# Two spectral-mixing and MLP layers: stores of made weight parts on ScalarE's DMA queue, issued two product steps after the part is complete, with the raw loads behind them

## The chip, the cores and the metric

One core of a Trainium2 chip runs the whole program. The metric is device time in microseconds of one execution; the kernel before was run three times. TensorE is called PE, VectorE DVE, ScalarE ACT, GpSimd POOL and SyncE SP in the profile. SP does no arithmetic here: it only issues DMAs.

## The reference, cut to what matters

```python
# x [2048, 576]; w1 [576, 4608]; w2 [4608, 576]; everything f32
def A(y):                                  # spectral mixing
    a, b = y @ dft_hid_re.T, y @ dft_hid_im.T
    return dft_seq_re @ a - dft_seq_im @ b
def B(y):                                  # MLP, gelu in its tanh form
    return gelu(y @ w1 + b1) @ w2 + b2
x = x + A(layernorm(x))
x = x + B(layernorm(x))
x = x + A(layernorm(x))
x = x + B(layernorm(x))
```

The two layers use the same w1, w2 and DFT matrices.

## The kernel before

**Products.** Each large matrix product is cut in 2 x 2 blocks and computed by a scheme of seven block products in place of eight (numbered 1 to 7; `ORDER` is the order in which a group of seven runs). For this, sums and differences of blocks are formed on both sides ("parts"). Each operand of TensorE is then split in two fp32r numbers, a high part (a copy by ScalarE) and a low part (the operand less the high part, a subtraction by VectorE), and a product is three passes of matmuls: high x high, high x low, low x high. A *part* of a weight is therefore a tile in `R` that holds high and low, and it has to be made once: raw blocks are loaded, POOL forms the sum or difference, ScalarE writes the high part, VectorE the low part. The finished parts of w1 and w2 are stored to DRAM scratch (`w1s`, `w2s`, both called `w_parts` in the profile, w1_parts and w2_parts in the lists of instructions) and loaded again by the later halves, so that the making is paid for once, in the first layer. `R` is the store of fp32r tiles and `A` that of f32 tiles, `bank` is PSUM.

**Stages.** Each layer has a *sequence stage* (class `Sequence`; the DFT along 2048 rows: 14 tiles after two opening ones, seven products each, of 24 matmuls 128x288; method `run`, from L663), then, for each of two halves of the rows, `hidden` (the DFT along 576 columns, the residual, the layer norm, transposes by TensorE) and `mlp` (L1015). The halves are interleaved: the last transposes of `hidden` (generator `turn_y`, taken step by step from L998 to L1003) stand among the first products of `mlp`.

**The MLP.** w1 is worked in 18 steps q, w2 in 9 groups g. `inner(q)` runs seven products of seven matmuls 128x512, adds up their banks (VectorE, `add`, L193), and makes GELU (ScalarE) and the parts of its result. `outer(g, i)` runs product i of the second matrix, in two half products of 12 matmuls 128x288 (one for each result tile of 128x576). Iteration g of the loop does: first inner (q = 2g), first outer (products 1, 6, 5, 3 of group g-1), second inner (q = 2g+1), second outer (products 7, 4, 2 of group g-1). A counter `at` numbers the places of an iteration: 0 to 6 the products of the first inner, 7 to 14 the half products of the first outer, 15 to 21 the second inner, 22 to 27 the second outer. PE runs the matmuls in this order of the code; a half product's result is taken out of its bank by VectorE's L193 add.

**What is made in the background.** Two makers run beside this work, and both put instructions into the same ScalarE, VectorE and SP queues.

- `weights()` (L249 on) makes the 126 parts of w1, 7 for each of 18 q. It is a generator; a step n writes the low of part n-1 (`low`, one VectorE subtraction L196, and at once the store of 128x640 and, in four of seven steps, the load of a raw block for q+1, 128x384) and the high of part n (`high`, L269 and L270 on ScalarE). Its parts lie in a ring `stage` of three slots, `n % 3`. `pump()` takes one step. `tick(3)` after each product of the first sequence stage (L694) pumps after three products of four; `tick(2)` in `inner` (L1161) after every second product; and `load_w` (L1030), which loads a w1 part for the MLP, pumps until that q's parts are made.
- `make(g)` (L1055), used only in the first half of the first layer (`first`), makes the seven w2 parts of group g: `hi` on ScalarE (L1061), `lo` on VectorE (L196, 128x576) with its store of 128x1152 behind it, then POOL's next difference and, in four of seven, the raw load for the next group (`load_raw`, L1051). A table of places says when: parts 1, 5, 6 at 0 to 5 (the first inner), 3 at 9 and 10, and 7, 4, 2 at 15 to 20 (the second inner). `advance()` (L1083) runs what is due at a place.

```python
        def low(n):
            ...
            sub(nc.vector, t[:, 0:5:2], cut(src), t[:, 1:4].bitcast(F32))
            dma(w1s[q, i - 1], at(n).bitcast(F32))
...
            return list(zip((0, 1, 2, 3, 4, 5, 9, 10, 15, 16, 17, 18, 19, 20),
                            one + five + six + three + seven + four + two))
```

**The DMA queue.** `dma` (L189, L190) is `nc.sync.dma_start`: all loads and stores of the kernel, 1347 of them, are issued by SP, in the order of the code. An issue waits in SP for whatever its tile or its data need, and all later issues wait behind it. Eight semaphores (DMAHW0 to DMAHW7 in the lists) are taken in turn, and an issue also waits for the earlier one that has its semaphore.

**The second layer's sequence stage** is prepared in pieces while the first layer's last MLP half still runs: `prepare` and `fill` (generators; L327 to L462) are moved on by `next(before)` in the last six inners (L1163). A piece loads, normalizes, or writes highs (ScalarE, L499 to L511) or lows (VectorE).

## Time and profile before

| what | value |
| --- | --- |
| median of three runs | 2736.05 us (2735.36 to 2740.49) |
| the profiled execution's own time | 2739.99 us |
| its span, first to last instruction | 2737.9 us |
| granted clock of TensorE, mean | 0.996 |
| PE busy (matmul) | 2669.0 us, 97% |
| PEld busy (weight load, beside PE) | 2500.1 us, 91% |
| DVE busy | 1772.6 us, 65% |
| ACT busy | 1101.3 us, 40% |
| POOL busy | 790.6 us, 29% |
| DMA | 544.91 MB, mean 199 GB/s |
| the first layer's sequence stage, about | 60 to 390 us |
| its first MLP half (w2 is made), about | 455 to 910 us |
| the second layer's sequence stage begins at about | 1350 us |

How to read it: a line of the groups has the code line, engine, operation, written tile <- read tiles, shape and count, then the busy time and the mean of one in ns, then the idle time of that engine just before these instructions with what ended most of it. TensorE's waits are listed as "who waits <- what released it: total us, count, longest". Rows of the chain of waits start with a time and a duration; SPq is SP's DMA issuing. Rows of the timeline read: start, duration, engine, line, instruction; a count x stands for that many instructions put together, and a bracket holds the wait ahead of it. In the stretches each engine has busy time and count, in the order PE, PEld, DVE, ACT, POOL, and then the granted clock, the share of the DMA engines' time and GB/s. DMA rows end with the median us from issue to landing.

### The profile page before, as it was taken

How to read it: one execution, taken by the hardware profiler on the slowest of the kernel's cores; microseconds unless marked ns; L12 is line 12 of the kernel's file. 1: busy time of each engine (PE TensorE's matmuls, PEld its weight loads, DVE VectorE, ACT ScalarE, POOL GpSimd, SP SyncE). 2: the span in 40 equal slices, each digit the busy share in tenths (PEclk: the TensorE clock that was granted, in tenths of full speed). 3: DMA queues.
4: the chain of work that ended last, by engine and by line, in shares of the span. 5: the costliest groups of instructions: out<-in, count | busy, mean ns of one | idle time of the engine just before them, and what ended most of it. 6: DMA issues, size and time to landing. Idle time of an engine off the chain costs nothing.

```text
span 2737.9 us, 45326 instructions
## 1 busy us (share of the span) xinstructions
PE 2669.0 (97%) x17488; PEld 2500.1 (91%) x17488; DVE 1772.6 (65%) x2582; ACT 1101.3 (40%) x1838; POOL 790.6 (29%) x746
## 2 busy tenths in 40 slices
PE   7999999999999999999999999999999999999999
PEld 7999998788888988988899999998989899898988
DVE  8788866777776575556566666565555556655555
ACT  6555545544443243333344333344333324433331
POOL 5222224543534432213241000042222224222222
PEclk9999999999999999999999999999999999999999
DMA  5666675777777546667463333536666673666664
GB/s 201 233 224 223 227 259 189 268 263 269 270 259 254 201 153 193 191 197 222 156 220 120 122 124 122 201 104 209 193 194 193 195 256 129 200 193 195 192 194 153
DMA packets 209286, 544.91 MB, mean 199 GB/s; under 512 B 22048, under 2 KB 56864, under 8 KB 208928
## 3 DMA queue, kind: packets, MB, share of 16 engines
q1 hardware_dynamic: 209072, 542.02, 60.2%
q8 instruction: 138, 2.26, 0.3%
q14 instruction: 76, 0.62, 0.1%
HBM read 429.87 MB, written 114.72 MB: 199 GB/s over the span
## 4 chain that ended last, share of the span: by engine, by line
PE 68%; DVE 5%; issue 3%; DMA 3%; POOL 2%; ACT 1%; SPq 0%; POOLq 0%; DVEq 0%; ACTq 0%
PE bank L203 67%; DVE R L196 2%; DMA R<-w_parts 2%; DVE A L193 1%; PE bank L818 1%; POOL A L196 1%; DVE A L196 1%; DVE bank L193 1%; POOL R L196 0%; DMA A<-in_c 0%; DMA w_parts<-R 0%; SPq L190 0%; ACT R L1179 0%; DVE moments L233 0%; ACT A L243 0%
## 5 line engine op out<-in xcount | busy, mean ns | idle before, releaser
L203 PE MATMUL bank<-R 128*128 128x288 f32 (+2 forms) x16972 | 2621.7, 316 | 56.1 <-DVE A L193 14.4
L203 PEld LDWEIGHTS bank<-R 128*128 128x128 f32 x16972 | 2445.8, 189 | 222.2 <-DVE A L193 24.2
L193 DVE TENSOR_TENSOR A<-bank,A 128x576 f32<-128x576 f32 (+3 forms) x808 | 566.7, 709 | 555.3 <-PE bank L203 473.0
L196 POOL TENSOR_TENSOR R<-A,R 128x512 fp32r<-128x512 f32 x288 | 374.5, 1311 | 951.8 <-ACT R L1179 912.2
L196 DVE TENSOR_TENSOR R<-A,R 128x1024 fp32r<-128x1024 f32 (+10 forms) x521 | 495.5, 975 | 61.0 <-ACT R L615 25.5
L193 POOL TENSOR_TENSOR A<-A 128x576 f32<-128x576 f32 (+2 forms) x102 | 135.9, 1334 | 633.0 <-ACT A L653 350.2
L1117 ACT ACTIVATE bank<-bank,b1t 128x512 f32<-128x512 f32 (+1 forms) x224 | 144.7, 646 | 372.0 <-DVE bank L193 256.5
L1179 ACT ACTIVATE R<-A 128x512 fp32r<-128x512 f32 x288 | 176.1, 629 | 279.0 <-DVE A L196 118.1
L615 ACT ACTIVATE R<-A 128x1024 fp32r<-128x1024 f32 x196 | 204.0, 1054 | 135.3 <-DVE A L196 105.9
L193 DVE TENSOR_TENSOR bank<-bank,A 128x512 f32<-128x512 f32 (+1 forms) x228 | 152.0, 669 | 151.1 <-PE bank L203 150.8
L196 DVE TENSOR_TENSOR R<-bank,R 128x512 fp32r<-128x512 f32 x336 | 210.1, 639 | 56.9 <-ACT R L199 48.0
L196 POOL TENSOR_TENSOR A<-A 128x384 f32<-128x384 f32 (+2 forms) x154 | 194.4, 1270 | 180.4 <-DVE R L196 90.9
L196 DVE TENSOR_TENSOR A<-A 128x1024 f32<-128x1024 f32 (+3 forms) x132 | 136.6, 1040 | 6.1 <-ACT A L243 2.1
L1144 ACT ACTIVATE A<-bank 128x512 f32<-128x512 f32 (+1 forms) x76 | 43.7, 575 | 233.2 <-PE bank L203 230.5
L1179 ACT ACTIVATE R<-bank 128x512 fp32r<-128x512 f32 x216 | 120.6, 596 | 32.9 <-PE bank L203 32.9
L196 DVE TENSOR_TENSOR A<-bank,A 128x512 f32<-128x512 f32 x144 | 97.9, 680 | 0.0
L199 ACT ACTIVATE R<-bank 128x512 fp32r<-128x512 f32 (+1 forms) x112 | 50.4, 492 | 92.6 <-PE bank L818 85.1
L243 ACT ACTIVATE A<-A,moments 128x576 f32<-128x576 f32 x64 | 53.7, 863 | 57.4 <-POOL moments L226 28.4
L655 DVE SCALAR_TENSOR_TENSOR A<-A 128x288 f32<-128x288 f32 x28 | 18.4, 657 | 88.8 <-POOL A L193 88.8
L1117 ACT ACTIVATE A<-bank,b1t 128x512 f32<-128x512 f32 (+1 forms) x76 | 50.5, 664 | 52.9 <-DVE bank L193 52.8
L270 ACT ACTIVATE R<-A,power,middle 128x128 fp32r<-128x128 f32 x126 | 60.8, 483 | 0.0
L269 ACT ACTIVATE R<-A 128x256 fp32r<-128x256 f32 x126 | 51.3, 407 | 14.0 <-DMA A<-in_w 10.8
(58 smaller groups left out, 613.6 us busy)
## 6 DMA issues: line engine op xcount, KB each, us to landing
R<-w_parts SPq DMA_DIRECT2D x504, 320.0 KB, 3.4
R<-w_parts SPq DMA_DIRECT2D x189, 576.0 KB, 3.7
A<-in_cs SPq DMA_DIRECT2D x112, 512.0 KB, 4.3
w_parts<-R SPq DMA_DIRECT2D x126, 320.0 KB, 4.0
w_parts<-R SPq DMA_DIRECT2D x63, 576.0 KB, 3.9
uv_mid<-A SPq DMA_DIRECT2D x32, 576.0 KB, 2.8
A<-in_w SPq DMA_DIRECT2D x72, 192.0 KB, 3.9
R<-dh_parts SPq DMA_DIRECT2D x23, 576.0 KB, 8.2
```

Source lines behind the costliest of these rows:

```text
L193: engine.tensor_tensor(dst, a, b, op=op)
L196: engine.tensor_tensor(dst, a, b, op=OP.subtract)
L199: nc.scalar.activation(hi, src, AF.Copy)
L203: nc.tensor.matmul(o, a, b, start=start, stop=stop, skip_group_check=True)
L243: nc.scalar.activation(dst, src, AF.Identity, bias=mv[:, 4:5], scale=mv[:, 3:4])
L269: nc.scalar.activation(t[:, 1:4:2], src[:, 0:3:2], AF.Copy)
L270: nc.scalar.activation(t[:, 2], src[:, 1], AF.Identity, bias=power[:, 2:3], scale=middle)
L615: nc.scalar.activation(self.cells[t, i](2, NP, P)[:, 0], self.source(t, i), AF.Copy)
L818: nc.tensor.transpose(at, v[:, k], ident)
L1117: nc.scalar.activation(dst, src, AF.Gelu_apprx_tanh, bias=bias(f))
L1144: nc.scalar.activation(up, o, AF.Copy)
L1179: nc.scalar.activation(H[q, k](2, TC)[:, 0], src, AF.Copy)
```

## The change

It has five parts.

1. **w1 stores.** A new helper `put` issues a DMA from ScalarE's queue. In `weights()` the store, the raw load (still SP) and the note that a q is made move out of `low(n)` into `keep(n)`, which runs two steps later: step n now runs `keep(n-2)`, `low(n-1)`, `high(n)`. The ring still has three slots.
2. **w1 steps in the sequence stage.** `tick(3)` becomes `pump()` after every product but product 2: six steps for seven products, 84 of the 126 in the stage where there were 73 or 74.
3. **w2 parts.** In `make` stores and raw loads go through `soon`: into a list `kept`, issued by `advance` two places later, stores through `put`. Parts 1 and 5 of the next group are made at places 24 to 27 of the iteration before (in the second outer), 6 at 0 and 1, 3 at 9 and 10, and 7, 4, 2 at 15 to 20 as before. For the first group 1, 5 and 6 stay together (0 to 5); the last group's 6, 3, 7, 4, 2 stand at 5 to 14.
4. **Pieces of the second sequence stage.** `high_parts` is cut in `high_left` and `high_z`, `low_parts(1)` in `low_z` and `right_sums`, with yields between; `lv` becomes a list of blocks, and the load of the second pair's left block leaves earlier.
5. **Last transposes.** The steps of `turn_y(3)` taken between the first MLP products are 0, 3, 3 where they were 1, 2, 3.

```diff
@@ -189,6 +189,9 @@
+    def put(dst, src):
+        nc.scalar.dma_start(dst, src)
+
     def add(engine, dst, a, b, op=OP.add):
@@ -275,9 +278,13 @@
             sub(nc.vector, t[:, 0:5:2], cut(src), t[:, 1:4].bitcast(F32))
-            dma(w1s[q, i - 1], at(n).bitcast(F32))
             if then:
                 then()
+
+        def keep(n):
+
+            q, k = divmod(n, 7)
+            put(w1s[q, steps[k][0] - 1], at(n).bitcast(F32))
             if k in (2, 4, 5, 6):
@@ -286,8 +293,10 @@
         yield
-        for n in range(7 * NQ + 1):
-            if n:
+        for n in range(7 * NQ + 2):
+            if n > 1:
+                keep(n - 2)
+            if 0 < n <= 7 * NQ:
                 low(n - 1)
@@ -351,7 +360,7 @@
                     yield
-            self.lv = Block(A, EARLY_X[2], 8 * P)(1, 8, P)
+            self.lv = [Block(A, EARLY_X[2], 8 * P)(8, P)]
             self.load_left(0)
@@ -370,23 +379,25 @@
                     yield
-                self.high_parts(0)
+                self.high_left(0)
+                yield
+                self.high_z(0)
                 yield
                 self.low_left(0)
+                self.lv = self.left_blocks()
+                self.load_left(1)
                 yield
...
                 yield
-            self.lv = Block(A, L_AT, NP * 8 * P)(NP, 8, P)
             if self.early:
                 self.t = Block(A, EARLY_T, 2 * D)
-                self.load_left(1)
-                yield
                 self.right_sums(0)
...
             else:
+                self.lv = self.left_blocks()
                 self.has_left(1)
@@ -418,9 +429,12 @@
                     self.low_left(1)
+                    yield
                     self.low_sums(0)
                     yield
-                    self.low_parts(1)
+                    self.low_z(1)
+                    yield
+                    self.right_sums(1)
                     yield
@@ -433,7 +447,11 @@
                         self.load_left(k)
-                if p + 1 < NP:
+                if p == 0 and self.early:
+                    self.high_left(1)
+                    yield
+                    self.high_z(1)
+                elif p + 1 < NP:
                     self.high_parts(p + 1)
@@ -460,6 +478,11 @@
+        def left_blocks(self):
+
+            v = Block(A, L_AT, NP * 8 * P)(NP, 8, P)
+            return [v[:, p] for p in ((0, 2, 1, *range(3, NP)) if self.early else range(NP))]
+
         def has_left(self, k):
@@ -484,7 +507,7 @@
             for t in range(PLAIN):
-                dma(self.lv[:, p, 4 * t:4 * t + 4], c0[p][:, t])
+                dma(self.lv[p][:, 4 * t:4 * t + 4], c0[p][:, t])
@@ -496,14 +519,17 @@
         def high_left(self, p):
-            nc.scalar.activation(self.left(p)[:, 0], self.lv[:, p], AF.Copy)
+            self.parts[p] = self.own.take()
+            nc.scalar.activation(self.left(p)[:, 0], self.lv[p], AF.Copy)
...
+            self.high_left(p)
+            self.high_z(p)
+
+        def high_z(self, p):
+
             v, z = self.x[p], self.Z[p](7, 2, DH)
-            if p not in self.parts:
-                self.parts[p] = self.own.take()
-                self.high_left(p)
             if p not in self.normal:
@@ -525,7 +551,7 @@
             c = self.left(p)
-            sub(nc.vector, c[:, 1], self.lv[:, p], c[:, 0].bitcast(F32))
+            sub(nc.vector, c[:, 1], self.lv[p], c[:, 0].bitcast(F32))
@@ -691,7 +717,8 @@
                     hidden.begin(self, ORDER.index(i))
-                tick(3)
+                if i != 2:
+                    pump()
             for k in range(2):
@@ -996,7 +1023,7 @@
         y_steps = turn_y(3)
-        for n in (1, 2, 3):
+        for n in (0, 3, 3):
             next(mlp)
@@ -1043,7 +1070,7 @@
-        due = []
+        due, kept = [], []
         if first:
@@ -1063,24 +1090,28 @@
                 sub(nc.vector, t[:, :, 1], src, t[:, :, 0].bitcast(F32))
-                dma(w2s[g, i - 1], got2[g, i](2, 2 * DH).bitcast(F32))
+                b = got2[g, i]
+                soon(lambda: put(w2s[g, i - 1], b(2, 2 * DH).bitcast(F32)))
+
+            def soon(step):
+                kept.append((at[1] + 2, step))
...
             six = [lambda: hi(6, x), lambda: (lo(6, x), sub(pool, x, b21, x))]
-            five = [lambda: hi(5, b11), lambda: (lo(5, b11), load_raw(g + 1, 0))]
-            three = [lambda: hi(3, b22), lambda: (lo(3, b22), sub(pool, b12, b22, b12), load_raw(g + 1, 2))]
-            seven = [lambda: hi(7, b12), lambda: (lo(7, b12), load_raw(g + 1, 1))]
+            five = [lambda: hi(5, b11), lambda: (lo(5, b11), soon(lambda: load_raw(g + 1, 0)))]
+            three = [lambda: hi(3, b22), lambda: (lo(3, b22), sub(pool, b12, b22, b12), soon(lambda: load_raw(g + 1, 2)))]
+            seven = [lambda: hi(7, b12), lambda: (lo(7, b12), soon(lambda: load_raw(g + 1, 1)))]
             four = [lambda: hi(4, x), lambda: lo(4, x)]
-            two = [lambda: hi(2, b21), lambda: (lo(2, b21), load_raw(g + 1, 3))]
-            if g == NG - 1:
-                return list(zip((1, 2, 5, 6, 7, 8, 9, 10, 12, 13, 14, 15, 16, 17),
-                                one + six + five + three + seven + four + two))
-            return list(zip((0, 1, 2, 3, 4, 5, 9, 10, 15, 16, 17, 18, 19, 20),
-                            one + five + six + three + seven + four + two))
-
-        at = [0]
+            two = [lambda: hi(2, b21), lambda: (lo(2, b21), soon(lambda: load_raw(g + 1, 3)))]
+            late = (5, 6, 7, 8, 9, 10, 11, 12, 13, 14) if g == NG - 1 else (0, 1, 9, 10, 15, 16, 17, 18, 19, 20)
+            return list(zip((24, 25, 26, 27), one + five)), list(zip(late, six + three + seven + four + two))
+
+        at = [0, 0]
         def advance(to=None):
+            at[1] += to is None
+            while kept and kept[0][0] <= at[1]:
+                kept.pop(0)[1]()
             while due and due[0][0] <= (at[0] if to is None else to):
@@ -1251,7 +1282,14 @@
             if first and g:
-                due.extend(make(g - 1))
+                if g == 1:
+                    soon, late = make(0)
+                    due.extend((n, step) for n, (_, step) in enumerate(soon))
+                    late[:2] = [(n + 4, step) for n, step in late[:2]]
+                due.extend(late)
+                if g < NG:
+                    soon, late = make(g)
+                    due.extend(soon)
             if g == NG:
@@ -1274,6 +1312,8 @@
                         outer(g - 1, i, 1 - f)
+        for _, step in kept:
+            step()
         for s in (c2, tmps):
```

In the MLP's group 4, second inner, SP's rows read before (lines L190 are the helper `dma`; the last row is the load of the w1 part for the inner's seventh product):

```order
L190 DMA w1_parts<-R_66 128x640 [waits DMAHW0_49,DVE_49]
L190 DMA A_67<-in_w1 128x384 [waits DMAHW1_49]
L190 DMA R_66<-w1_parts 128x640 [waits DMAHW2_49,PE_49]
L190 DMA w2_parts<-R_66 128x1152 [waits DMAHW3_49,DVE_49]
L190 DMA A_67<-in_w2 128x2x288 [waits DMAHW4_49]
L190 DMA R_66<-w1_parts 128x640 [waits DMAHW5_49,PE_49]
```

After the change the same place of SP's queue, with the same load as the last row:

```order
L190 DMA A_67<-in_w1 128x384 [waits DMAHW2_49,DVE_49]
L190 DMA R_66<-w1_parts 128x640 [waits DMAHW3_49,PE_49]
L190 DMA R_66<-w1_parts 128x640 [waits DMAHW5_49,PE_49]
L190 DMA A_67<-in_w2 128x2x288 [waits DMAHW0_49,DMAHW4_49,DVE_49,Pool_49]
L190 DMA R_66<-w1_parts 128x640 [waits DMAHW1_49,PE_49]
L190 DMA R_66<-w1_parts 128x640 [waits DMAHW7_49,DMAHW3_49,PE_49]
```

Both stores have left SP's queue, and the raw load of w2 (in_w2) no longer stands directly ahead of the load; another w1 load stands between.

On ScalarE, in the first sequence stage, one product's rows before (L269 and L270 are `high`, L615 and L645 the stage's own work):

```order
L645 ACTIVATE A_67<-bank_68 128x288 [waits DVE_49,PE_49]
L269 ACTIVATE R_66<-A_67 128x2x128 [waits DMAHW4_49,Pool_49]
L270 ACTIVATE R_66<-A_67,power_70,middle_72 128x128 [waits Activation_49]
L615 ACTIVATE R_66<-A_67 128x1024 [waits Activation_49]
L269 ACTIVATE R_66<-A_67 128x2x128 [waits DMAHW5_49,DMAHW7_49,DVE_49,Activation_49]
```

and after (L193 is now `put`; `high` is L272 and L273):

```order
L193 DMA w1_parts<-R_66 128x640 [waits DVE_49,Activation_49]
L272 ACTIVATE R_66<-A_67 128x2x128 [waits DMAHW6_49,Pool_49]
L273 ACTIVATE R_66<-A_67,power_70,middle_72 128x128
L641 ACTIVATE R_66<-A_67 128x1024 [waits DVE_49]
L193 DMA w1_parts<-R_66 128x640 [waits Activation_49]
L272 ACTIVATE R_66<-A_67 128x2x128 [waits DMAHW1_49,Pool_49]
```

The store of a part stands in ScalarE's own queue now, ahead of the next high, and that high waits for a DMA semaphore.

On VectorE, at the end of an iteration (second outer) and the start of the next one's first inner, before (L193 the adds out of the banks, L196 subtractions):

```order
L196 TENSOR_TENSOR R_66<-bank_68,R_66 128x512
L196 TENSOR_TENSOR A_67<-bank_68,A_67 128x512 [waits DVE_49]
L193 TENSOR_TENSOR A_67<-bank_68,A_67 128x576 [waits PE_49]
L196 TENSOR_TENSOR R_66<-bank_68,R_66 128x512 [waits Activation_49]
L196 TENSOR_TENSOR A_67<-A_67,bank_68 128x512
L193 TENSOR_TENSOR A_67<-bank_68,A_67 128x576 [waits PE_49] x2
```

and after (the same helpers are L196 and L199):

```order
L199 TENSOR_TENSOR R_66<-bank_68,R_66 128x512
L199 TENSOR_TENSOR A_67<-bank_68,A_67 128x512 [waits DVE_49]
L199 TENSOR_TENSOR R_66<-A_67,R_66 128x2x288 [waits DMAHW0_49,Activation_49]
L196 TENSOR_TENSOR A_67<-bank_68,A_67 128x576 [waits PE_49]
L199 TENSOR_TENSOR R_66<-bank_68,R_66 128x512 [waits Activation_49]
L199 TENSOR_TENSOR A_67<-A_67,bank_68 128x512
L196 TENSOR_TENSOR A_67<-bank_68,A_67 128x576 [waits PE_49]
L199 TENSOR_TENSOR R_66<-A_67,R_66 128x2x288 [waits DMAHW7_49,Activation_49]
L196 TENSOR_TENSOR A_67<-bank_68,A_67 128x576 [waits PE_49]
```

The two rows of 128x2x288 are the lows of w2 parts 1 and 5 of the next group; they stood in the next iteration's first inner.

## The prediction

> **What bounds the kernel now.** I read the page first, then TensorE's waits, the chain of waits, busy time by stretch, and last the timeline at the places where TensorE stood.
>
> ```profile
> span 2737.9 us, 45326 instructions
> L203 PE MATMUL bank<-R 128*128 128x288 f32 (+2 forms) x16972 | 2621.7, 316 | 56.1 <-DVE A L193 14.4
> L615 ACT ACTIVATE R<-A 128x1024 fp32r<-128x1024 f32 x196 | 204.0, 1054 | 135.3 <-DVE A L196 105.9
> L270 ACT ACTIVATE R<-A,power,middle 128x128 fp32r<-128x128 f32 x126 | 60.8, 483 | 0.0
> L269 ACT ACTIVATE R<-A 128x256 fp32r<-128x256 f32 x126 | 51.3, 407 | 14.0 <-DMA A<-in_w 10.8
> ```
>
> The matmul line stands idle for 56.1 us of 2737.9, so TensorE is the bound and no change of waits can win more than some 2%. Where those waits lie:
>
> ```profile
> PE bank L203 <- DMA R<-w_parts: 8.6, 9, 2.4
> PE bank L203 <- DVE A L193: 8.1, 13, 1.1
> PE bank L203 <- DVE bank L193: 7.1, 7, 2.2
> ...
> 653.26 9.01 PE bank L203 x49
> 701.88 9.01 PE bank L203 x49
> 1154.44 45.22 PE bank L203 x266
> ...
> 100.00:390.00 290.00, 290.00 (x2199) 290.00 (x2198) 239.98 (x268) 158.35 (x285) 69.14 (x51) 1.00 0.68 231
> 455.00:860.00 405.00, 379.30 (x2170) 333.43 (x2171) 296.39 (x436) 198.60 (x381) 180.80 (x136) 1.00 0.73 258
> 860.00:910.00 50.00, 45.38 (x305) 42.60 (x304) 31.24 (x43) 12.31 (x23) 20.19 (x14) 0.97 0.87 320
> ```
>
> The first three are TensorE's waits between 455 and 910 us, the stretch of the first MLP half, which makes the w2 parts while it works. From the chain: the same point of two neighbouring groups is 701.88 - 653.26 = 48.6 us apart, while a group of a later half, which only loads its parts, takes 45.22. So about 3.4 us a group, over eight groups, is what making costs there. The stretches (PE, PEld, DVE, ACT, POOL busy, clock, DMA share) say the opposite of 100 to 390 us: PE is busy for all 290 us, with the same weights() steps beside it. DVE is at 83% there and ACT at 55%.
>
> **The change part by part.** Own time of the profiled execution: 2739.99 us, for a span of 2737.9. The median of the runs is 2736.05, 3.94 lower; I sum against 2739.99 and take 3.94 off.
>
> *Stores off SP's queue.* In each group TensorE waits once for a w1 part, at the last product of the second inner:
>
> ```profile
> 658.85 0.41 SPq L190 DMA_DIRECT2D R<-w_parts  x1
> 661.38 0.32 SPq L190 DMA_DIRECT2D w_parts<-R  x1
> 661.75 0.43 SPq L190 DMA_DIRECT2D A<-in_w  x1
> 662.27 0.90 SPq L190 DMA_DIRECT2D R<-w_parts  x1
> ...
> 667.23 21.18 PE L203 MATMUL bank<-R 128*128 128x512 f32 x121 [0.89 <-DMA R<-w_parts]
> ...
> R<-w_parts SPq DMA_DIRECT2D x100, 320.0 KB, 4.9
> w_parts<-R SPq DMA_DIRECT2D x51, 576.0 KB, 3.8
> w_parts<-R SPq DMA_DIRECT2D x45, 320.0 KB, 5.0
> ```
>
> The last three rows are transfers of 500 to 860 us with their median time to landing. The load issued at 662.27 is the one waited for until 667.23: 4.96 us, the usual 4.9. It stood in SP's line behind a store that waits for a VectorE low (661.38) and a raw load. SP was free after 658.85 + 0.41 = 659.26, and the product that frees the slot ended near 659.7, so it could have left 2.5 us earlier; even at 4.9 us it would then land near 664.6, before it is wanted. After the change neither store nor raw load stands there until two product steps later. Of 8.6 us I take 7.5 as gone. Bounds: nothing (the landing stretches by as much), and all 8.6.
>
> What the Trainium skill says against this: "DMA: Bandwidth & Descriptors", section "Issuing engines are not separate DMA queues", holds that transfers started by different engines run on the same 16 DMA engines, so that another issuing engine saves only the sequencer's issue time. By it the 7.5 us would be no gain at all. The rows speak for a second effect, SP's order, which the rule does not cover; a second queue's landing times no run here shows.
>
> *w2 parts 1 and 5 a half group earlier, eleven w1 steps moved into the sequence stage.* The other two waits of a group:
>
> ```profile
> 689.26 6.89 PE L203 MATMUL bank<-R 128*128 128x512 f32 x43 [0.85 <-DVE bank L193]
> 696.74 2.54 PE L203 MATMUL bank<-R 128*128 128x288 f32 x17 [0.59 <-DVE A L193]
> ...
> 675.80 0.75 DVE L193 TENSOR_TENSOR A<-bank,A 128x576 f32<-128x576 f32 x1
> 677.06 0.68 DVE L196 TENSOR_TENSOR A<-A,bank 128x512 f32<-128x512 f32 x1
> 677.65 0.75 DVE L193 TENSOR_TENSOR A<-bank,A 128x576 f32<-128x576 f32 x1
> 685.93 2.67 DVE L196 TENSOR_TENSOR R<-A,R 128x576 fp32r<-128x576 f32 x2
> 692.81 0.69 DVE L193 TENSOR_TENSOR bank<-bank,A 128x512 f32<-128x512 f32 x1
> L196 DVE TENSOR_TENSOR R<-A,R 128x576 fp32r<-128x576 f32 x63 | 62.1, 988 | 3.7 <-ACT R L1061 3.7
> ```
>
> Both come from one VectorE backlog in the first inner, which holds three w2 lows (parts 1, 5, 6) and three w1 lows: at 685.93 two lows take 2.67 us, and the bank add of the inner's last product starts only at 692.81, two microseconds after its matmuls. With two of the three w2 lows gone, I take 4.5 of the 7.1 us of bank waits as gone (the longest, 2.2, is in the first group, whose parts 1, 5, 6 stay together) and 4 of the 8.1 us of A waits. Groups 6 to 8 also lose their w1 steps, since 84 instead of 73 or 74 of the 126 are done in the sequence stage (six of seven products instead of three of four). There PE has no idle time, DVE grows by 11 lows of about 0.8 us to 86%, so I cost them at nothing. Bounds: 0 and 15.2.
>
> Where they go is not free. In the second outer VectorE has no gap left at its fifth half product: that add runs 677.65 to 678.40, and PE, which ran from 667.23 through seven products of 1.6 us and 72 matmuls of 0.132, wants these banks at about 678.4. The low of part 1 now stands ahead of the fourth half product's add (675.80), so the fifth's moves back by one low, 0.99 us (the last row; 1.33 as a pair at 685.93). Eight groups: **+8 us**. Bounds: 0, if VectorE catches up, and 8 x 1.33 = 10.6. That wait is the next one to be late where the old ones go.
>
> *The last group* has 50.00 - 45.38 = 4.6 us of idle PE, in which parts 1 and 5 are still made. They are ready now: -2.5, between 0 and -4.6.
>
> *What the stores cost ScalarE.* 189 issues at SP's 0.32 us are 60 us, under an engine busy for 198.6 of 405 us in the MLP stretch: hidden as issues. But the staging ring has three slots. Before, a store left right after its low and its slot was refilled two steps on; now the store of step n-2 leaves in step n, and step n+1 refills that slot. The fill (L269) is in the same ScalarE queue, so ScalarE stands until the store has landed. With S the issue time, L the landing, and 0.41 + 0.48 + 1.05 + about 0.23 (a bank copy in four steps of seven) = 2.17 us of work between stores, a step takes max(2.5, (L + 2.17) / 2). In the sequence stage a product is 24 x 290/2199 = 3.17 us; seven less the one without a step leave (22.2 - 1.3) / 6 = 3.48 us, so **L up to 4.8 us is free**.
>
> ```profile
> w_parts<-R SPq DMA_DIRECT2D x71, 320.0 KB, 3.4
> ...
> A<-in_x SPq DMA_DIRECT2D x32, 288.0 KB, 5.4
> ```
>
> In 60 to 390 us these stores land in 3.4: cost nothing. At 5.4 (the page's x loads, the nearest slower row) a step takes 3.79, which is 0.31 x 6 x 14 tiles = **26 us** lost. In the MLP two products give 3.2 us between steps, and 5.0 us of landing makes ScalarE late by up to 2 us in the inner with four steps; its highs are then late for VectorE, whose bank add has 1.6 - 0.7 us to spare. Queued behind the waiting fill are GELUs and highs, then the lows. I take 0.8 us in each of the five groups that still have w1 steps: **+4**, between 0 and 5 x 2.4 = 12.
>
> *Second sequence stage.* Between 1345 and 1460 us:
>
> ```profile
> PE bank L203 <- DVE A L193: 5.2, 2, 2.9
> ...
> 1358.37 1.06 ACT L499 ACTIVATE R<-A 128x1024 fp32r<-128x1024 f32 x1
> 1359.32 0.92 ACT L509 ACTIVATE R<-A 128x864 fp32r<-128x864 f32 x1
> 1360.14 0.44 ACT L511 ACTIVATE R<-A 128x288 fp32r<-128x288 f32 x1
> ```
>
> 2.4 us of one piece stand ahead of the MLP's highs. The new yields split it in two, and the second pair's left load leaves earlier: -3.5, between 0 and -5.2. The later pieces move back by two, into VectorE's wait for x_mid loads, at no cost.
>
> *Order of the last transposes* (four halves):
>
> ```profile
> 979.98 0.66 PE L931 MATMUL bank<-ident,A 128*128 128x128 f32 x4 [1.40 <-ACT A L243]
> ...
> 985.74 0.51 PE L203 MATMUL bank<-R 96*128 96x256 f32 x2 [0.73 <-DVE R L196]
> ```
>
> Seven more matmuls of 0.12 us now fill 0.84 of the 1.40 us, but VectorE's splits set the end at 985.74: -1, between 0 and -3.4.
>
> **Sum:** -7.5 - 4.5 - 4 + 8 - 2.5 + 4 - 3.5 - 1 = **-11 us**. 2739.99 - 11 = 2729, less 3.94: **2725 us**, with 2717 to 2730 as this case's own range.
>
> **Rivals.** *More is won*: VectorE catches up and ScalarE's stalls fall in its idle half, so neither +8 nor +4 comes: -23, 2713. For it: VectorE stands 0.28 to 2 us at several points of each group. Against: none of them lies just ahead of the fifth add.
>
> *Loads land no sooner*: the rule above, as a mechanism here: ScalarE's transfers and SP's share the DMA engines (share 0.73), and 4.9 us grows to over 7. The 7.5 is not won: -3.5, 2732.5. Against: the bytes are the same.
>
> *ScalarE's stalls reach VectorE in every inner with w1 steps*: +12 for +4, -3, 2733.
>
> *Slower: the ring binds the sequence stage.* One mechanism, L269 waiting for the store one step back; it decides from L = 4.8 us on, and from (11 + 5.5) / 84 x 2 = 0.4 us above it the whole is slower than before. At 5.4: 2725 + 26 = 2751. For it: the x loads' 5.4 and the 5.0 us in the MLP; the store now competes with cs loads instead of following them. Against: 3.4 us now.
>
> **How the numbers follow.** Chances: forecast 0.36, more won 0.20, loads no sooner 0.06, stalls in every inner 0.10, slower 0.26 (0.20 the ring, the rest a place I have not priced), 0.02 a mixture on the fast side. A difference of 0.2%, 5.5 us, is about what can be told from no change. Faster by more (under 2730.6): 0.36 + 0.20 + 0.02 = 0.58; within: 0.16; slower: 0.26. The range reaches from under "more won" to the ring's price: 2706 to 2752.
>
> **What would show it.** Right: in 455 to 910 us the wait for R<-w_parts under 2 us, the bank waits near 2.5, a new wait for an L196 add (L193 before) at the first product of a group's first inner; groups 6 to 8 near 46 us apart; PE still busy all of 100 to 390. Wrong: PE idle in 100 to 390 with ScalarE's fill waiting for w_parts<-R (the ring), R<-w_parts landing over 6 us (shared engines), or bank waits over 7 us in the second inner (the stalls).

## The result, and the profile after

The changed kernel takes 2770.19 us (median of 4 runs, 2769.08 to 2771.25) against 2735.7: ratio 1.0118, 95% interval 1.0105 to 1.0131. It is **34 us slower**, where 11 us faster was forecast. The profiled execution took 2770.94 us.

The page after, then the waits between 455 and 910 us (who waits <- what released it: total us, count, longest). The code lines have moved: L206 is the matmul (L203 before), L196 the add (L193), L199 the subtraction (L196), L193 the new `put`, L272 and L273 the high of a w1 part (L269, L270), called "fill" below:

```profile
span 2768.8 us, 45214 instructions
L206 PE MATMUL bank<-R 128*128 128x288 f32 (+2 forms) x16972 | 2632.1, 317 | 79.2 <-DVE A L196 48.7
L272 ACT ACTIVATE R<-A 128x256 fp32r<-128x256 f32 x126 | 52.0, 413 | 113.7 <-DMA w_parts<-R 67.4
...
ACT R L272 <- DMA w_parts<-R: 56.9, 20, 6.2
PE bank L206 <- DVE A L196: 37.9, 15, 4.6
PE bank L206 <- DVE bank L196: 1.1, 1, 1.1
PE bank L206 <- DMA R<-w_parts: 0.7, 1, 0.7
```

The two waits that were to go are gone: 0.7 us for R<-w_parts (8.6 before), 1.1 for the bank adds (7.1 before). But the wait for VectorE's A adds has grown from 8.1 to 37.9 us, and ScalarE's fill, which waited 14 us in the whole program before, waits 113.7.

To see where, compare the same matmuls. Every trace has 17488 of them in nearly the same order, so the start of the 3251st and of the 5701st cut out the same work in each: the last transposes and the nine groups of the first MLP half, "the stage" from here on. The stretch of each kernel (PE, PEld, DVE, ACT, POOL busy, granted clock, DMA share, GB/s), before and then after:

```profile
447.00:898.20 451.20, 421.49 (x2452) 372.84 (x2451) 330.94 (x484) 210.85 (x400) 199.78 (x150) 0.99 0.74 261
```

```profile
446.40:931.00 484.60, 434.86 (x2452) 389.45 (x2452) 313.19 (x473) 200.58 (x378) 187.96 (x144) 0.95 0.66 234
100.00:390.00 290.00, 289.77 (x2196) 289.54 (x2195) 245.04 (x280) 168.56 (x306) 87.25 (x57) 1.00 0.73 245
```

The stage takes 33.4 us more, with no engine busier but PE and its weight loads, and PE's clock is lower. The sequence stage (last row) is as full as before. Cut by matmul number:

| matmuls | what | before | after |
| --- | --- | --- | --- |
| 0 to 3250 | first sequence stage and `hidden` | 434.9 | 434.9 |
| 3250 to 5700 | first MLP half | 451.2 | 484.6 |
| 5700 to 8500 | second half | 457.2 | 457.4 |
| 8500 to 9250 | into the second sequence stage | 113.7 | 111.3 |
| 9250 on | the rest | 1261.7 | 1262.2 |

Within the stage, pieces of 250 matmuls that hold w1 steps take 54.4, 54.4 and 55.1 us where they took 44.7, 45.0 and 45.6; once the w1 steps are done, 44.0 and 44.3 where they took 46.7 and 46.3.

One of the stalls, read backwards. The timeline of after around 640 us (start, duration, engine, line, instruction; the idle time ahead and its releaser in brackets):

```profile
636.89 0.35 ACTq L193 DMA_DIRECT2D w_parts<-R  x1
640.88 0.33 ACTq L193 DMA_DIRECT2D w_parts<-R  x1
641.25 0.69 ACT L1148 ACTIVATE A<-bank,b1t 128x512 f32<-128x512 f32 x1 [2.56 <-DVE A L196]
641.33 0.36 ACTq L193 DMA_DIRECT2D w_parts<-R  x1
643.49 0.42 ACT L272 ACTIVATE R<-A 128x256 fp32r<-128x256 f32 x1 [1.54 <-DMA w_parts<-R]
644.19 0.64 ACT L1148 ACTIVATE bank<-bank,b1t 128x512 f32<-128x512 f32 x1
644.76 1.07 ACT L1210 ACTIVATE R<-bank 128x512 fp32r<-128x512 f32 x2
...
640.11 0.76 DVE L196 TENSOR_TENSOR A<-bank,A 128x576 f32<-128x576 f32 x1 [0.45 <-PE bank L206]
645.38 0.69 DVE L199 TENSOR_TENSOR R<-bank,R 128x512 fp32r<-128x512 f32 x1 [4.51 <-ACT R L1210]
645.99 2.01 DVE L196 TENSOR_TENSOR A<-bank,A 128x512 f32<-128x512 f32 x3
...
647.38 5.87 PE L206 MATMUL bank<-R 128*128 128x288 f32 x26 [4.12 <-DVE A L196]
```

TensorE waits 4.12 us for the adds that empty its banks (645.99). VectorE had stood 4.51 us for ScalarE's highs (644.76), and these stand in ScalarE's queue behind a GELU, the fill (643.49) and two store issues (640.88, 641.33). ScalarE first stood 2.19 us until 640.88, with nothing to do but issue a store: that left 0.08 us behind the landing (640.80) of a part's load that SyncE had issued at 633.65. The bracket of the GELU behind it names the add that ended at the same time. Then the fill stood until the store of the first row had landed, 6.51 us after its issue. Nine such stalls lie between 528 and 762 us, two in most groups.

The chain of waits names the same loop (start, us, what):

```profile
574.08 4.46 DMA R<-w_parts
578.61 6.61 DMA w_parts<-R
587.80 1.35 DVE A L196 x2
589.20 12.13 PE bank L206 x57
602.18 5.50 DMA A<-in_w
607.75 5.21 DMA w_parts<-R
616.02 1.36 DVE A L196 x2
617.42 14.60 PE bank L206 x81
```

A store leaves ScalarE at 578.61, 0.08 us behind the landing of the load issued at 574.08; its own landing then holds a fill. ScalarE stands ahead of a store issue, over 0.3 us, at 30 places of the stage. At 22 of them the store leaves 0.08 us behind the landing of a transfer with no data in common: 11 loads of parts (20.4 us), 8 raw loads (14.7), 3 earlier stores. The trace shows why: at each of the 22 that transfer had the same one of the eight semaphores as the store, and for the 19 loads it was SyncE that had issued it. So an issue waits for the earlier DMA that has its semaphore, whichever engine issued that one. At the other eight places a subtraction of VectorE ends last.

### The profile page after: what moved, and what is told of

The parts are those of the page before. It is cut to its first block, busy times and chain, and to the rows that moved or that the text cites. A ratio compares the mean times of both kernels' runs of the same rounds, so it can differ in the third digit from the quotient of the medians.

```text
span 2768.8 us, 45214 instructions
## 1 busy us (share of the span) xinstructions
PE 2680.9 (97%) x17488; PEld 2514.4 (91%) x17488; DVE 1762.7 (64%) x2582; ACT 1100.6 (40%) x1838; POOL 797.3 (29%) x746
## 4 chain that ended last, share of the span: by engine, by line
PE 69%; DMA 4%; DVE 4%; issue 2%; ACT 1%; POOL 1%; SPq 0%; ACTq 0%; DVEq 0%; POOLq 0%
PE bank L206 68%; DMA w_parts<-R 3%; DVE R L199 2%; DVE A L196 1%; PE bank L845 1%; DMA R<-w_parts 1%; DVE A L199 1%; POOL A L199 0%; DMA A<-in_w 0%; POOL R L199 0%; ACT R L1210 0%; DVE moments L236 0%; ACT bank L1148 0%; DVE bank L196 0%; ACT A L246 0%
## 5 line engine op out<-in xcount | busy, mean ns | idle before, releaser
L206 PE MATMUL bank<-R 128*128 128x288 f32 (+2 forms) x16972 | 2632.1, 317 | 79.2 <-DVE A L196 48.7
L206 PEld LDWEIGHTS bank<-R 128*128 128x128 f32 x16972 | 2459.9, 190 | 243.2 <-DVE A L196 62.3
L196 DVE TENSOR_TENSOR A<-bank,A 128x576 f32<-128x576 f32 (+3 forms) x808 | 566.9, 710 | 559.0 <-PE bank L206 479.7
L199 POOL TENSOR_TENSOR R<-A,R 128x512 fp32r<-128x512 f32 x288 | 379.2, 1328 | 937.1 <-ACT R L1210 868.8
L199 DVE TENSOR_TENSOR R<-A,R 128x1024 fp32r<-128x1024 f32 (+8 forms) x521 | 481.1, 946 | 63.3 <-ACT R L641 27.4
L196 POOL TENSOR_TENSOR A<-A 128x576 f32<-128x576 f32 (+2 forms) x102 | 134.9, 1327 | 553.4 <-ACT A L679 367.2
L199 POOL TENSOR_TENSOR A<-A 128x384 f32<-128x384 f32 (+2 forms) x154 | 198.8, 1291 | 299.8 <-DVE R L199 181.2
L199 DVE TENSOR_TENSOR R<-bank,R 128x512 fp32r<-128x512 f32 x336 | 210.0, 640 | 92.8 <-ACT R L202 49.2
L196 DVE TENSOR_TENSOR bank<-bank,A 128x512 f32<-128x512 f32 (+1 forms) x228 | 152.4, 670 | 154.0 <-PE bank L206 153.8
L199 DVE TENSOR_TENSOR A<-A 128x1024 f32<-128x1024 f32 (+3 forms) x132 | 141.8, 1079 | 6.1 <-ACT A L246 2.1
L199 DVE TENSOR_TENSOR A<-bank,A 128x512 f32<-128x512 f32 x144 | 97.9, 680 | 0.0
L272 ACT ACTIVATE R<-A 128x256 fp32r<-128x256 f32 x126 | 52.0, 413 | 113.7 <-DMA w_parts<-R 67.4
L273 ACT ACTIVATE R<-A,power,middle 128x128 fp32r<-128x128 f32 x126 | 60.6, 481 | 0.0
```

Of the source, the lines that this page charges most:

```text
L196: engine.tensor_tensor(dst, a, b, op=op)
L199: engine.tensor_tensor(dst, a, b, op=OP.subtract)
L206: nc.tensor.matmul(o, a, b, start=start, stop=stop, skip_group_check=True)
L272: nc.scalar.activation(t[:, 1:4:2], src[:, 0:3:2], AF.Copy)
L273: nc.scalar.activation(t[:, 2], src[:, 1], AF.Identity, bias=power[:, 2:3], scale=middle)
```

## The experiments

"Stage" is the time of the same 2450 matmuls, 451.2 us before and 484.6 after the change; it comes from one trace each, without the spread of whole runs. Ratios are to the kernel before, with 95% intervals.

**Which part: the w1 steps or the rest.** `c` puts weights() and tick(3) back as before the change; `d` puts only the w1 part into the kernel before.

```diff
 # c_w1_as_before
             sub(nc.vector, t[:, 0:5:2], cut(src), t[:, 1:4].bitcast(F32))
+            dma(w1s[q, i - 1], at(n).bitcast(F32))
...
-                if i != 2:
-                    pump()
+                tick(3)
 # d_w1_only (against the kernel before)
-            dma(w1s[q, i - 1], at(n).bitcast(F32))
...
+        def keep(n):
...
+            put(w1s[q, steps[k][0] - 1], at(n).bitcast(F32))
...
```

> The changed kernel with weights() and its three pumps of four products as before the change (store at once, SyncE's queue); w2 parts a half group earlier, their late stores on ScalarE, the pieces of the second sequence and the transposes stay changed. Theory that all of the loss is in the w1 steps: what is left of the change is a gain, as in its groups without w1 steps (-2.7 and -2.0) and its second sequence (-2.4): 2718 to 2733. Rival: the w2 lows ahead of the outer adds are what makes VectorE late (the +8 of the forecast, repeated at two places of a group): 2740 to 2760.

> The kernel before with the w1 part of the change alone: store and raw load two steps later, on ScalarE's queue, and six steps for seven products in the sequence stage. Theory that the loss is in the w1 steps: 2762 to 2785, with ScalarE waiting 50 us or more for w_parts<-R in the first MLP half. Rival, that the loss needs the w2 parts beside it (their stores on the same queue, or their lows): 2733 to 2745.

Measured: `c` 2739.82 us, 1.0011 (1.0002 to 1.002), stage 451.3. `d` 2753.55, 1.0068 (1.0051 to 1.0085), stage 467.0. So the loss needs the w1 part, but that alone makes half of it: both expectations missed, `c` by the gain that did not come, `d` by size.

**How much per w1 step.** `g` is the change with tick(3): eleven more w1 steps in the stage.

```diff
-                if i != 2:
-                    pump()
+                tick(3)
```

> The changed kernel with tick(3) in the sequence stage again, so that 10 or 11 more w1 steps fall in the first MLP half. Theory that each group with w1 steps pays about 9.5 us: 1.5 more groups, +14 us, 2778 to 2792. Rival, that the loss there is of the w2 parts and not of the w1 steps: 2766 to 2774.

Measured: 2777.26, 1.0153 (1.0137 to 1.0169), stage 489.1. Seven more, not fourteen: more steps, more loss, at half the rate.

**Which queue, which store.** `a` puts both kinds of stores on SyncE, `e` only the w2 stores, `f` only the w1 stores; all stay two steps late.

```diff
 # a_stores_sp
-        nc.scalar.dma_start(dst, src)
+        nc.sync.dma_start(dst, src)
 # e_w2_stores_sp
-                soon(lambda: put(w2s[g, i - 1], b(2, 2 * DH).bitcast(F32)))
+                soon(lambda: dma(w2s[g, i - 1], b(2, 2 * DH).bitcast(F32)))
 # f_w1_stores_sp
-            put(w1s[q, steps[k][0] - 1], at(n).bitcast(F32))
+            dma(w1s[q, steps[k][0] - 1], at(n).bitcast(F32))
```

> The changed kernel with both kinds of stores back on SyncE's queue, everything else as changed (still two steps later). Ring theory: in the first MLP half ScalarE's high of a w1 part (L272) waits for the landing of the store that was issued only one step before, from whichever queue; so the stalls stay: L272 waits for w_parts<-R 40 us or more in the first MLP half, TensorE waits for the L196 adds there about 35 us, time 2755 to 2775. Rival, the queue theory: it is the second queue that makes the landing longer (6.1 us for a w1 store, 5.0 before) and the issues that delay ScalarE; then landing is back at 5.0, the L272 wait below 15 us and the time 2725 to 2738.

> The changed kernel with only the w2 stores back on SyncE's queue (still two places later); the w1 stores stay on ScalarE's. Theory that a w1 store lands late because it follows a 576 KB w2 store on the same queue: the wait of L272 for w_parts<-R in the first MLP half falls from 57 us to about the 18 us of the kernel with the w1 part alone, time 2740 to 2752. Rival, that the w1 stores alone make it (the store stands in the same queue as the high that waits for it, so each late high makes the next store late): the wait stays over 40 us, time 2760 to 2772.

> The changed kernel with only the w1 stores back on SyncE's queue (still two steps later); the w2 stores stay on ScalarE's. Theory of the loop on ScalarE (a late high issues the next store late, whose landing makes the high after the next late): the loop is cut, the L272 wait falls to 30 us or less as with both stores on SyncE, time 2738 to 2750. Rival, that ScalarE's w2 stores make the delay: 2758 or more.

Measured: `a` 2747.37, 1.0041 (1.0026 to 1.0056), stage 453.5; `e` 2738.73, 1.0007 (0.9997 to 1.0017), stage 451.7; `f` 2747.03, 1.0042 (1.0026 to 1.0057), stage 455.1. So in the stage: both on ScalarE +33.4, the w1 stores alone +0.5 (`e`), the w2 stores alone +3.9 (`f`), none +2.3 (`a`). The two are bad only **together**, and the whole runs say the same: `a`, `e` and `f` lie 23 to 31 us under the change. None of the three went as it was argued. `a` falls between its two theories, and in `e` and `f` the fill still waits 34.9 and 32.7 us for stores, where about 18 and at most 30 were expected; the loss in the stage went all the same. The waits of `e` in the stage:

```profile
ACT R L272 <- DMA w_parts<-R: 34.9, 19, 5.0
PE bank L206 <- DVE A L196: 16.1, 16, 2.2
ACT R L272 <- DMA A<-in_w: 12.3, 3, 5.3
```

47 us of fill waits, and TensorE's wait is 16.1 in place of 40.1 in the same stage. In `e`, ScalarE does not stand once over 0.3 us ahead of a store issue. The traces of `a` and `f` show another loss, 3.1 and 4.9 us up to matmul 3250. There, in the first sequence stage, w1 stores on SyncE land in 4.8 and 4.9 us, on ScalarE's queue in 3.0. The trace of `a` is that of its fastest run, 6.2 us under its median, so where the rest of its 11 us goes is not shown. In the MLP the queue makes no such difference: the same stores land in 6.0 us in `a` and in 6.1 after the change. Rows of DMA issues from 60 to 390 us, then from 447 us to the end of the stage, each for `a` and then for after:

```profile
w_parts<-R SPq DMA_DIRECT2D x81, 320.0 KB, 4.8
```

```profile
w_parts<-R ACTq DMA_DIRECT2D x81, 320.0 KB, 3.0
```

```profile
w_parts<-R SPq DMA_DIRECT2D x45, 320.0 KB, 6.0
```

```profile
w_parts<-R ACTq DMA_DIRECT2D x45, 320.0 KB, 6.1
```

**The ring.** `b` issues the w1 store (and raw load) right behind the next high, one step earlier; `h` also takes no w1 step in the last tile of the sequence stage.

```diff
 # b_one_step
-            if n > 1:
-                keep(n - 2)
...
             if n < 7 * NQ:
                 high(n)
+            if n:
+                keep(n - 1)
...
 # h_one_step_no_tail, besides
-                if i != 2:
+                if i != 2 and t < NT - 1:
                     pump()
```

> The changed kernel with the w1 store and raw load issued right behind the high of the next part, one step earlier than in the change and still on ScalarE's queue. Ring theory: the slot is now refilled two steps after its store's issue, 6.4 us in the MLP; the L272 wait in the first MLP half falls from 57 us to under 10, the groups with w1 steps lose their +9.5 us, time 2722 to 2735. Queue theory: the stores' landing stays at about 6 us and ScalarE waits for VectorE's low ahead of each issue besides; time 2755 or more.

> The kernel with the w1 store one step earlier (b_one_step) that takes no w1 step in the last tile of the sequence stage, where its store waits for VectorE's low and keeps the highs of the hidden stage behind it on ScalarE. Theory: the 5.4 us lost at the end of the sequence stage there go, six steps move to the first MLP half for 2 us at most; 2731 to 2739, against 2741.9. Rival, that the loss at the end of the sequence stage has another cause: 2741 or more.

Measured: `b` 2741.89, 1.002 (1.0011 to 1.003), stage 448.6, fill waits 3.2 us. `h` 2739.3, 1.0011 (1.0001 to 1.002), stage 454.2. `b` missed its time, 2735 at most, and met its fill waits. The ring's hold is a part of the cause: released a step earlier, the stage is shorter than before the change. (`b` moves the raw load too; `m`, below, moves that alone and keeps a stage of 473.7.) What `b` loses lies in the last tile of the sequence stage: ScalarE's timeline there has

```profile
379.00 0.35 ACTq L193 DMA_DIRECT2D w_parts<-R  x1
379.40 1.83 ACT L806 ACTIVATE R<-R 128x576 fp32r<-128x576 f32 x3 [2.74 <-DVE A L196]
```

an issue that waits for a fresh low and holds the hidden stage's highs. `h` takes that away (matmul 3250 starts at 446.2 us, in `b` at 452.1) and gives the gain back in the stage, 5.6 us for six more steps there, where at most 2 were expected.

**The raw loads.** `l` is `e`, `m` is the change, both with the w1 raw loads at once behind the low.

```diff
             if then:
                 then()
+            if k in (2, 4, 5, 6):
+                load(q + 1, (2, 4, 5, 6).index(k))
...
-            if k in (2, 4, 5, 6):
-                load(q + 1, (2, 4, 5, 6).index(k))
```

> The kernel with the w2 stores on SyncE (e_w2_stores_sp) and the w1 raw loads at once behind the low, as before the change; w1 stores still two steps later on ScalarE. Theory: the 22 us in which the high of a q's second part waits for its raw block, now one step ahead, go from ScalarE, but TensorE had lost little by them: 2734 to 2739. Rival, that they still cost TensorE the +1.5 of the middle groups: 2728 to 2733.

> The changed kernel with only the w1 raw loads at once behind the low again; both kinds of stores two steps later on ScalarE. Theory that the stores on ScalarE's queue (the ring and the waits ahead of their issue) make the loss: 2758 to 2772. Rival, that the late raw load, which the changed kernel's longest waits only hide behind a store, is the larger part: below 2750.

Measured: `l` 2732.99, 0.9993 (0.9984 to 1.0002), stage 448.2; `m` 2760.04, 1.0089 (1.0075 to 1.0103), stage 473.7. The late raw load costs too: 10 us of the change's 34 go with it, 3.5 us of `e`'s stage. The part that it serves is the second of a q, whose high then comes one step, not two, behind the load; in the change its fill waits up to 6.2 us, and what lands last there is mostly a store, in `e` three times of five the raw load. `l` met its rival and not its theory: TensorE had lost by that wait.

**Why only together.** `i` and `p` lay ScalarE work at the places of `e`'s w2 stores (63 copies of 0.68 us; two copies at each of the 36 places in an inner); they compute the same. `q` issues an inner's w2 stores (and raw loads) behind the w1 step of the same place; `o` puts those stores on SyncE.

```diff
 # i (and p, with 2 copies if i in (5, 6, 7, 4))
...
+                    top = b(2, 2, DH)[:, :, 0]
+                    nc.scalar.activation(top, top.bitcast(F32), AF.Copy)
...
 # q_w1_first
...
-                    advance()
+                    advance(hold=True)
                     tick(2)
+                    flush()
 # o_inner_w2_sp
-                soon(lambda: put(w2s[g, i - 1], b(2, 2 * DH).bitcast(F32)))
+                soon(lambda: (dma if i in (5, 6, 7, 4) else put)(w2s[g, i - 1], b(2, 2 * DH).bitcast(F32)))
```

> The kernel with the w2 stores on SyncE (e_w2_stores_sp), and at the place of each w2 store a copy of the part's high onto itself on ScalarE (63 copies of 128x576, 0.68 us each, 43 us in all). The DMAs stay those of e. Theory that ScalarE's lost time is the price, whatever loses it (57 us of fill waits and 42 us of waits ahead of store issues in the changed kernel, 47 us in e, which the slack swallows): 43 us more of it bring the loss back, 2752 to 2772. Rival, that the loss is in the transfers (w1 stores landing later behind w2 stores on one queue): no copy changes that, 2736 to 2744.

> The kernel with the w2 stores on SyncE (e_w2_stores_sp), and at the four places of a group where such a store falls in an inner, two copies of that part's high onto itself on ScalarE (36 places, 1.37 us each, 49 us in all). Theory (1), lumps of ScalarE's time ahead of a fill: 2758 to 2775. Theory (2), the landing of stores on one queue: not over the 2745.6 of the spread dose.

> The changed kernel with the w2 stores and raw loads of an inner issued behind the w1 step of the same place and not ahead of it; both on ScalarE's queue as changed. Theory (1): a wait ahead of a w2 store no longer delays the w1 store and fill of its place, but still the highs behind: 2745 to 2760. Theory (2): the w1 store no longer follows a w2 store, its landing falls from 6.8 to about 5.5 us, and the loss goes: 2738 to 2745. Neither, the sum of waits counts wherever they stand: 2763 to 2772.

> The changed kernel with the w2 stores that fall in an inner (parts 5, 6, 7, 4) on SyncE's queue; those in an outer (1, 3, 2) and all w1 stores stay on ScalarE's. Theory that the loss needs a w2 store ahead of a w1 fill in the same inner: the first MLP half is 450 to 457 us (matmuls 3250 to 5700) against 484.6, time 2737 to 2745. Rival, that any 63 or 27 stores more on the queue do it in proportion: 2752 to 2760.

Measured: `i` 2745.61, 1.0035 (1.0021 to 1.0049), stage 461.7; `p` 2749.93, 1.0054 (1.004 to 1.0068), stage 459.7; `q` 2750.52, 1.0053 (1.004 to 1.0067), stage 462.0; `o` 2737.27, 1.0007 (0.9998 to 1.0017), stage 449.5. `o` shows where: without the 36 w2 stores of the inners on ScalarE's queue the loss is gone, though the 27 of the outers are still on it. `q` keeps the number of stores and shows that their place ahead of the fill is two thirds of it (22.6 of 33.4 us). That moving any 36 of the 63 stores would do as `o` did is not excluded; no run moves the 27 alone. The doses miss their lower bound, and `p` lies between its two theories: ScalarE's time there costs 8 to 10 us, not 33, so time alone is not all. Nor is it the same loss. TensorE's wait for the A adds is 13.2 us in `i` and 16.8 in `p`, about the 16.1 of `e` and not the 40.1 of the change; what grew is its wait for loaded parts, from 3.8 to 10.7 and 9.3. Its waits in the stage of `p`:

```profile
PE bank L206 <- DVE A L196: 16.8, 16, 2.4
PE bank L206 <- DMA R<-w_parts: 9.3, 7, 1.8
```

All of it in one table: ScalarE's idle time over 0.3 us just ahead of a fill and just ahead of a store issue, summed over the stage of each trace.

| kernel | ahead of fills | ahead of stores | sum | stage less 451.2 |
| --- | --- | --- | --- | --- |
| before | 9.6 | 0 | 9.6 | 0 |
| l | 20.5 | 1.6 | 22.1 | -3.0 |
| c | 2.8 | 20.1 | 22.9 | +0.1 |
| e | 47.0 | 0 | 47.0 | +0.5 |
| a | 48.1 | 0 | 48.1 | +2.3 |
| b | 3.2 | 53.6 | 56.8 | -2.6 |
| o | 44.4 | 12.8 | 57.2 | -1.7 |
| f | 50.0 | 11.7 | 61.8 | +3.9 |
| h | 6.5 | 56.1 | 62.5 | +3.0 |
| q | 20.2 | 46.6 | 66.8 | +10.8 |
| m | 24.8 | 52.0 | 76.8 | +22.5 |
| after | 34.4 | 49.0 | 83.5 | +33.4 |
| g | 39.3 | 62.9 | 102.3 | +37.9 |

Up to some 60 us are swallowed; from 62.5 to 83.5 us each microsecond goes with about one and a half of loss, and in `g` 18.8 us more go with only 4.5. This is an order of the kernels, not a price shown: with their copies counted, `i` and `p` have 85 and 88 us and lose 10.5 and 8.4. `d` stands outside too: 38.5 us cost it 15.8. It lacks the w2 lows moved out of the first inner, so this move may be what makes the slack; no run tests it by itself with the late w1 steps, and without them (`c`) it won nothing.

**Versions that could win.** `k` keeps everything on SyncE, w1 stores and raw loads at once, w2 stores two places later; `n` is `l` with the transposes as before.

```diff
 # both
-        for n in (0, 3, 3):
+        for n in (1, 2, 3):
...
```

> Nothing on ScalarE's queue: w1 store and raw load at once on SyncE as before the change, w2 stores and raw loads two places later on SyncE, w2 parts 1 and 5 a half group earlier, six w1 steps for seven products in the sequence stage, pieces of the second sequence as changed, transposes as before. Theory: no fill waits and no issue waits on ScalarE, the gains of the groups without w1 steps (-2.7, -2.0) and of the second sequence (-2.5 to -4.5) stay: 2724 to 2733. Rival, that w1 loads on SyncE wait behind the stores again and take it back: 2734 to 2740.

> The kernel with w2 stores on SyncE and w1 raw loads at once (l_raw_early, 2733.0), with the transposes as before the change (1, 2, 3), which cost +0.6 us in each second half: 2730 to 2733, faster than before by 0.1 to 0.2%. Rival: the transposes' order is worth nothing there, 2733 to 2735.

Measured: `k` 2736.03, 1.0002 (0.9993 to 1.0011), stage 451.5: the rival. `n` 2731.81, **0.9983 (0.9974 to 0.9991)**, stage 445.0: faster than before by 0.17%, as expected. Its stage (same columns as above) and TensorE's waits in it:

```profile
447.30:892.40 445.10, 423.10 (x2453) 374.23 (x2452) 310.56 (x473) 202.23 (x378) 189.52 (x144) 0.99 0.72 255
PE bank L206 <- DVE A L196: 9.1, 11, 4.3
PE bank L206 <- DMA R<-w_parts: 3.5, 3, 1.2
PE bank L206 <- DVE bank L196: 1.1, 1, 1.1
```

## Why the prediction was wrong

The step that failed is the term **"What the stores cost ScalarE"**, +4 us in the MLP, bounded by 12. It priced a high that waits for a store; it left out that ScalarE also waits ahead of the store issues themselves, and that the raw loads come a step closer. The term measured about +38: the 33.4 us that the stage lost, and the 4.7 that its two pieces without w1 steps won (46.65 to 43.99 and 46.32 to 44.30) and these stalls hid. Point by point:

- *SP's order* (-7.5): the wait went from 8.6 to 0.7 us, but as a gain about 5 us are shown at most, for in the change TensorE itself comes later. In kernels whose stage is no more than 0.1 us longer than before, the wait is 5.0 us with both kinds of stores on ScalarE (`b`), 5.5 in `o` and 9.5 where only the w2 stores left SyncE (`c`); where only the w1 stores did (`d`) it is 11.6. With everything late and all on SyncE (`a`) it is 3.9, so a second queue is not needed for what was won. These are single traces, and `l` and `n`, alike but for the transposes, have 9.4 and 3.5. The loads landed in 5.4 us in the stage, 4.9 before: not over 7, as the rival "loads land no sooner" had it. The Trainium skill, "DMA: Bandwidth & Descriptors", section "Issuing engines are not separate DMA queues", says that starting DMAs from several engines saves only the sequencer's time to start them. The 3.9 us of `a`, beside the 3.8 of `e` with the w1 stores on ScalarE, agree with that.
- *VectorE's bank adds* (-4.5): right, 7.1 to 1.1 us, and 8.3 in `d`, which leaves the w2 lows where they were. The A waits (-4) cannot be told from the new stalls in the change; in `k`, which has none, they went from 7.3 to 4.9 us in the stage.
- *A new wait behind the fourth outer add* (+8): did not come. Where the w1 steps are done, all of TensorE's waits for VectorE's A adds between 764 and 860 us are 0.4 us, and from 500 us on no product of an inner waits for them in `k` and `n`.
- *The ring in the sequence stage* (free up to a landing of 4.8 us): the stores landed in 3.0, and TensorE was busy for 289.77 of 290 us. With the stores on SyncE (`a`) they landed in 4.8, the formula's edge, and TensorE lost 2.1 us of the 290: the formula fits there.
- *The ring in the MLP* (+4): the mechanism was named, its size taken from the stores' old landing, 5.0 us on SyncE. They landed in 6.1. That is not the queue's doing: the stores of `a` landed in 6.0 on SyncE. The high also waited for the raw load, now a step closer, which the term left out although that load moves in the same edit (`m`: 10 us). And ScalarE waits ahead of the store issues themselves: 49 us. That an issue waits for the earlier one with its semaphore stands in the description of the kernel before, and the term counted issues at 0.32 us each.
- *What a stall costs*: no loss of TensorE's clock was counted. Behind stalls of this length there is one (below). In the stage, the time between two matmuls' starts above the usual (0.131 us for 128x288, 0.229 for 128x512) that no wait explains grew by about 15 of the 33.4 us, from 10.0 to 24.7 where it is over 0.05 us each.
- *Second sequence stage* (-3.5): -2.4, and -4.3 to -4.9 in `n`, `c` and `l`. *Last group* (-2.5): its last 250 matmuls lost 0.3 us in the change and won 1.3 in `n`. *Transposes* (-1): +0.6 in each second half (43.78 to 44.38 us for the same 250 matmuls), and back at 43.78 in `k` and `n`.

The slower rival was this mechanism, a fill that waits for the store one step back, but laid in the sequence stage, where the steps are further apart (3.48 us, against 3.2 in the MLP) and the stores landed in 3.0. That its price there (26 us) is near the loss is an accident.

Shown, then, is what makes the loss (the w2 stores of the inners on ScalarE's queue, ahead of a fill that waits for a w1 store one step back), with the waits that it goes through. Open is why waits ahead of the w2 stores cost three times or more what equal ScalarE work costs. They end with loads which themselves wait until TensorE frees a slot, so a late TensorE makes ScalarE later; a fixed dose has no such loop. That fits, and no run shows it alone.

## What to carry to other kernels

A store that leaves an engine's own queue later holds its buffer longer: before moving one, work out the slot's way round (issue, landing, next fill) against the time between steps, with the landing measured where it will run, and do the same for each load that moves with it. An issue on a computing engine can be a wait, here of up to 3.0 us and not 0.3, when it shares semaphores with another engine's transfers. Put it where what stands behind it is not wanted soon (`q`), or leave it on the queue of an engine that computes nothing (`o`). Some such waiting was free here, and more was not: the two kinds of stores cost the stage 0.5 and 3.9 us alone and 33.4 together, so test edits that share a queue together as well as apart.

## What was not expected of the hardware

**The granted clock halves behind a stall.** PE, PEld, DVE, ACT, POOL, clock, DMA share in stretches of after:

```profile
640.00:647.00 7.00, 3.27 (x25) 3.03 (x23) 2.38 (x4) 4.21 (x9) 0.00 (x0) 0.89 1.03 411
647.40:651.90 4.50, 4.50 (x19) 4.50 (x20) 3.69 (x6) 0.52 (x2) 1.89 (x2) 0.50 0.02 6
652.00:662.00 10.00, 10.00 (x52) 8.64 (x51) 6.38 (x11) 4.16 (x9) 6.57 (x5) 0.99 0.62 211
...
761.18 5.10 PE L206 MATMUL bank<-R 128*128 128x288 f32 x25 [2.27 <-DVE A L196]
761.20:765.20 4.00, 4.00 (x19) 4.00 (x20) 3.39 (x6) 0.03 (x1) 1.41 (x1) 0.57 0.31 125
```

After the 4.12 us stall the clock is 0.50 for 4.5 us and TensorE is "busy" all the while; the profile's busy time hides this loss. The Trainium skill, "TensorE: Matmul & The Clock Gate", section "Part 1: The HAM clock gate (the "warmup" mystery)", says that an idle window of about 3.4 us halves the clock and that some 3.4 us of work restore it, with windows that run freely. The trace agrees on the half and, roughly, on the way back (4.5 us at 0.50, then 0.99); but here 2.27 us of waiting were enough (last two rows).

**A second queue landed sooner in one stage and not in the other.** The same w1 stores, 320 KB each and as late, landed in 3.0 us on ScalarE's queue and 4.8 on SyncE's in the sequence stage, and in 6.1 and 6.0 in the first MLP half, against 4.8 before the change, when they left at once behind the low. Why the sequence stage differs is open.
